# Six decay tiles spread by one-hot products into PSUM, products of zeros first, and a new order in the opening of an attention-then-FFN kernel

## The chip, the cores and the metric

One NeuronCore of a Trainium2 chip runs the whole program. The metric is device microseconds of one execution: the median of three runs before is 554.11 us (554.05 to 554.75). TensorE (PE) multiplies into PSUM, VectorE (DVE) and ScalarE (ACT) read and write SBUF and PSUM, GpSimd (POOL) works in SBUF, and SyncE (SP) issues nearly all transfers (DMAs), in the order of its queue.

## The reference

Three stages follow one another on 4 batches of 768 tokens:

1. A scan attention with 8 heads, 32 channels a head and a state of 16. With the decay `a` clipped to 1e-6..1, within a chunk `y[i] = sum over j<=i of (C_i . B_j) * prod(a[j+1..i]) * x_j`, plus `C_i . state` decayed to i; the state at the end of a chunk is the decayed old state plus the decayed sum of `B_j x_j`.
2. A first FFN on 256 channels: `h = max(x@w1, x@w2, x@w3)` (768 wide), then `h @ w_out`.
3. A second FFN: `(sigmoid(x@w_gate) * (x@w_val)) @ w_out` (1536 wide), output in float32.

All inputs are float32 or, for the weights, float64; the weights arrive as pairs of 32-bit words and are turned on the chip into a high and a low part of reduced float32.

## The kernel before, in words

The attention runs in 64 steps. A step `k` is one chunk `c = k // 8` of 96 tokens and one group `g = k % 8` of four (batch, head) units. `attention(k)` (L321) does for its step: on ACT a masked copy of C (L327, only in the first 16 steps), four float32 products `s` on PE (L332; from step 16 on bf16 products, L335), then on POOL and DVE the multiplication of `s` and of `bx` with the decay into `mt` (L340, L347), then four products `y` on PE (L356), each 32 columns of the array wide. After every fourth step ACT and DVE write `xt_hi` and `xt_lo` (L366, L368) and DVE transposes the new state into `xs` of the next chunk (L372). The first 12 steps (`START`) form the opening: only when `xt` of step 11 is written can the first FFN begin, on 512 tokens at a time.

The decay of two steps is one tile `dec{n}` (n = k // 2) of 8 units by 97 values, the same on all 128 partitions. `load_decay` (L267) transfers it from DRAM with a broadcast over the partitions, for n = 0 and 1 straight from the input, from n = 2 on from `ad`, a DRAM copy that `clip_all` (L256) has clipped and stored. Then `decay(n)` (L283) makes it into products of decays by two scans on DVE (L291), which multiply along each row and add the pattern `delta`, a constant of zeros and ones in PSUM (a copy of `delta_s` in SBUF). Four tiles exist at a time (`DECS`), so the transfer of tile n waits in SP's queue until the steps of tile n - 4 are done.

The weights of the first FFN come in twelve pieces (a00 to a51) of two 256 KB transfers. `BEHIND` says how many pieces are put in SP's queue behind the transfer of which decay tile. Each piece is decoded (L155 on) by three ACT instructions (L165, L170, L174), one on DVE (`t_a`, L178), two on POOL (L183, L213) and one more on ACT (L211).

The order on each engine is made by a planner that places instructions by its own estimate of when they are ready and by their order in the program; `tc.issue_after(i)` sets an instruction behind another on the same engine. `Pipe.tick` moves every open step and every open decode one stage on. In the first FFN a pass over 512 tokens has six blocks m (a piece pair each) of 18 products `u` and 6 products `o` (L406 to L408), 144 products of 512 columns in all; the steps 12 to 23 of the attention are spread over the first pass. In them the products `y` of four steps are issued together after the fourth (L353).

## Time and profile before

| | before |
|---|---|
| median of 3 runs | 554.11 us |
| time of the profiled execution | 554.77 us |
| its span, first to last instruction | 553.0 us |
| outside the span | 1.77 us |
| PE busy | 535.5 us (97%) |
| DVE, ACT, POOL busy | 384.0, 322.2, 128.2 us |
| moved by DMA | 50.5 MB |

All stretches named below are in microseconds from the start of the span. "Busy" is the time that instructions of an engine cover; the ends of PE's products are modelled, so its pace is best read from the distance between starts. PEclk is the granted TensorE clock as a share of 2.4 GHz; where the profile has no record of it, as in the first 43 us, the column shows 1.00. "PEld" is the loading of weights into PE's array, which overlaps the products. "x8" is the number of instructions that a row has merged.

### The profile page before, as it was taken

To read this page: it belongs to the slowest core of one execution; us is meant where nothing else is said; L and a number is where in the kernel's file an instruction comes from. 1 tells how busy PE (TensorE), PEld (TensorE's weight loads), DVE (VectorE), ACT (ScalarE), POOL (GpSimd) and SP (SyncE) were. 2 spreads that over 40 slices of the span, in tenths; PEclk is the share of its full clock that TensorE was granted. 3 is DMA by queue.
4 is the path that set the end of the run, shared out by engine and by line. 5 is a ranking of instruction groups with operands and counts; after the bars stand their busy time and mean duration, and the time that the engine had idled before them with its cause. 6 is when DMAs were issued, how large, how long until landed. Compare 5 with 4: busy or idle time off the path is not lost.

```text
span 553.0 us, 7923 instructions
## 1 busy us (share of the span) xinstructions
PE 535.5 (97%) x2885; PEld 429.3 (78%) x2885; DVE 384.0 (69%) x648; ACT 322.2 (58%) x571; POOL 128.2 (23%) x161
## 2 busy tenths in 40 slices
PE   5998999999999999999999999999999999999997
PEld 5777667777677778888888878877888878888885
DVE  4988985676776834799988896586455567554554
ACT  5667745334335223687798886675555565555563
POOL 3568996555555430000000000000000000000000
PEclk9999899999999999999999999999999999999999
DMA  7999985894985118013220000001000002000002
GB/s 234 344 268 241 298 200 87 187 180 142 192 197 125 31 59 321 1 38 118 76 75 0 1 1 2 0 19 58 1 0 2 0 1 77 0 1 0 1 0 76
DMA packets 32150, 50.51 MB, mean 91 GB/s; under 512 B 3184, under 2 KB 18160, under 8 KB 32112
## 3 DMA queue, kind: packets, MB, share of 16 engines
q1 hardware_dynamic: 31824, 49.63, 34.1%
q8 instruction: 22, 0.36, 0.3%
q10 hardware_dynamic: 288, 0.39, 0.2%
q14 instruction: 16, 0.13, 0.1%
HBM read 38.51 MB, written 3.25 MB: 76 GB/s over the span
## 4 chain that ended last, share of the span: by engine, by line
PE 83%; DMA 9%; DVE 4%; ACT 1%; issue 1%; SPq 0%; DVEq 0%; ACTq 0%
PE o L659 17%; PE ug L628 15%; PE uv L628 15%; PE u L406 9%; PE u L408 8%; PE u L407 8%; DMA raw_a<-in_w 6%; PE o L407 3%; PE o L406 3%; PE o L408 3%; DMA dec<-ad 2%; PE y L356 2%; PE s L335 1%; DVE dec L291 1%; DMA ad<-ac 1%
## 5 line engine op out<-in xcount | busy, mean ns | idle before, releaser
L659 PE MATMUL o<-hi,w_d 128*128 128x512 f32 x288 | 97.6, 390 | 0.0
L406 PE MATMUL u<-xt_hi,w_a 128*128 128x512 f32 x216 | 88.4, 409 | 3.7 <-DVE s L488 2.6
L628 PE MATMUL ug<-xt_hi,w_g 128*128 128x512 f32 x252 | 91.5, 392 | 0.1
L628 PE MATMUL uv<-xt_hi,w_v 128*128 128x512 f32 x252 | 90.3, 390 | 0.0
L407 PE MATMUL u<-xt_lo,w_a 128*128 128x512 f32 x216 | 85.8, 397 | 0.1
L408 PE MATMUL u<-xt_hi,w_a 128*128 128x512 f32 x216 | 85.5, 396 | 0.0
L659 PEld LDWEIGHTS o<-hi,w_d 128*128 128x128 f32 x288 | 54.0, 188 | 11.3 <-ACT hi L702 0.2
L703 DVE TENSOR_TENSOR lo<-y,hi 128x512 fp32r<-128x512 f32 x72 | 49.4, 688 | 16.8 <-ACT hi L702 15.9
L291 DVE TENSOR_TENSOR_SCAN dec<-dec,delta 128x388 f32<-128x388 f32 x64 | 57.8, 945 | 1.3 <-DMA dec<-ad 1.1
L477 ACT CAST hi<-s 128x512 fp32r<-128x512 f32 x36 | 22.3, 621 | 61.5 <-DVE s L488 60.9
L659 PE MATMUL o<-lo,w_d 128*128 128x512 f32 x144 | 56.4, 391 | 0.8 <-DVE lo L703 0.8
L628 PEld LDWEIGHTS ug<-xt_hi,w_g 128*128 128x128 f32 x252 | 47.3, 188 | 12.1 <-ACT ug L631 0.9
L628 PEld LDWEIGHTS uv<-xt_hi,w_v 128*128 128x128 f32 x252 | 47.3, 188 | 10.6 <-DVE y L699 0.8
L406 PEld LDWEIGHTS u<-xt_hi,w_a 128*128 128x128 f32 x216 | 41.2, 191 | 13.7 <-POOL mt L340 1.7
L628 PE MATMUL ug<-xt_lo,w_g 128*128 128x512 f32 x126 | 49.1, 390 | 0.0
L628 PE MATMUL uv<-xt_lo,w_v 128*128 128x512 f32 x126 | 49.0, 389 | 0.0
L408 PEld LDWEIGHTS u<-xt_hi,w_a 128*128 128x128 f32 x216 | 41.4, 192 | 9.1
L407 PEld LDWEIGHTS u<-xt_lo,w_a 128*128 128x128 f32 x216 | 41.3, 191 | 8.4 <-DVE xt_lo L368 0.6
L702 ACT CAST hi<-y 128x512 fp32r<-128x512 f32 x72 | 44.4, 620 | 5.8 <-DVE y L699 4.4
L699 DVE TENSOR_TENSOR y<-uv,y 128x512 f32<-128x512 f32 x36 | 24.8, 688 | 30.9 <-PE uv L628 30.7
L486 DVE TENSOR_TENSOR s<-u,s 128x512 f32<-128x512 f32 x36 | 24.8, 688 | 24.6 <-PE u L408 19.4
L636 DVE TENSOR_TENSOR y<-ug,y 128x512 f32<-128x512 f32 x36 | 24.8, 690 | 24.4 <-ACT y L633 17.4
(103 smaller groups left out, 956.9 us busy)
## 6 DMA issues: line engine op xcount, KB each, us to landing
dec<-ad SPq DMA_DIRECT2D x30, 388.0 KB, 5.8
raw_a<-in_w SPq DMA_DIRECT2D x18, 256.0 KB, 6.9
bi<-parts SPq DMA_DIRECT2D x36, 128.0 KB, 5.3
cs<-parts SPq DMA_DIRECT2D x36, 96.0 KB, 5.5
xs<-in_xh SPq DMA_DIRECT2D x6, 512.0 KB, 5.0
raw_g<-in_wg SPq DMA_DIRECT2D x6, 512.0 KB, 5.0
raw_v<-in_wv SPq DMA_DIRECT2D x6, 512.0 KB, 5.9
raw_d<-in_wo SPq DMA_DIRECT2D x6, 512.0 KB, 4.3
```

Source lines behind the costliest of these rows:

```text
L291: dve.tensor_tensor_scan(out=f, data0=f, data1=delta.rearrange("p u w -> p (u w)"), initial=0.0, op0=ALU.mult, op1=ALU.add)
L406: pe.matmul(ps, wlo, a_hi(k), start=k == 0, stop=False)
L407: pe.matmul(ps, whi, a_lo(k), start=False, stop=False)
L408: pe.matmul(ps, whi, a_hi(k), start=False, stop=k == kn - 1)
L477: act.copy(hl[0], s)
L486: dve.tensor_tensor(out=s, in0=banks[1], in1=s, op=ALU.max)
L628: turn[0] = pe.matmul(ps, w, x, start=new and e == 0, stop=e == 2, skip_group_check=not new)
L636: evict[1] = dve.tensor_tensor(out=self.t[k], in0=ps, in1=self.t[k], op=ALU.add)
L659: turn[0] = pe.matmul(acc2[t][d], w, x, start=n == 1 and e == 0, stop=n == M2 and e == 2)
L699: evict[1] = dve.tensor_tensor(out=g, in0=v, in1=g, op=ALU.mult)
L702: act.copy(hl[0], g)
L703: dve.tensor_tensor(out=hl[1], in0=g, in1=hl[0].bitcast(F32), op=ALU.subtract)
```

## The change

The six first decay tiles are no longer transferred. The decay input is loaded once, 64 rows of 4 units by 97 values into `a4`, and clipped; the other 64 rows are set to zero. `spread(h)` multiplies `a4` on PE by a matrix that is a column of `delta_s` with a single 1 in row h, the same for all 128 outputs, so that all 128 partitions of a PSUM bank hold row h of `a4`, half a decay tile. Two banks (`o0`, `o1`) are used in turn; product h + 2 follows the scan of h. The scan then reads this bank and `delta_s` and writes the tile in SBUF. Twelve products of zeros stand first on PE; eight more are written into the program behind steps 9, 10 and 11 (3, 3 and 2).

In the order: no transfer of tiles 0 to 5; the store of `ad` after the first `x`; two weight pieces right after the first transfers, then two behind each of tiles 6 to 10; the second half of `x` of chunk 1 and the `bc` of chunk 2 behind piece a01; tiles 6 and 7 are scanned after step 11 and after the DVE instruction of piece a10; the state's transposes of step 7 come after `xt_lo` of step 11; the DVE instructions of pieces a00, a01 and a10 are set behind the multiplications of steps 6, 7 and 11, those of the later pieces behind `xt_lo` of step 11; and in steps 12 to 23 each step issues its own products `y` (`SHARED` in place of `START`).

```diff
+LATER = START // 2
+IDLE0 = 12
+IDLE = {9: 3, 10: 3, 11: 2}
+AFTER = {"a00": 6, "a01": 7, "a10": 11}
+SPREAD = 6
-BEHIND = {4: 1, 5: 1, 6: 2, 7: 2, 8: 2, 9: 1, 10: 1, 11: 1, 12: 1}
+BEHIND = {6: 2, 7: 2, 8: 2, 9: 2, 10: 2}
...
-        with behind(1):
-            dve.scalar_tensor_tensor(out=t, in0=f1, scalar=3, in1=sg, op0=ALU.logical_shift_left,
-                                     op1=ALU.bitwise_or)
+        with behind(1) if second else tc.issue_after(mts[AFTER.get(name, -1)].ins):
+            mts[name] = dve.scalar_tensor_tensor(out=t, in0=f1, scalar=3, in1=sg,
+                                                 op0=ALU.logical_shift_left, op1=ALU.bitwise_or)
...
-        t = awk.tile([128, 2, LW], F32, tag="ac", bufs=1, name="ac")
+        t = a4[0:NC * NP * 2]
+        dve.memset(a4[NC * NP * 2:128], 0.0)
         sp.dma_start(out=t.rearrange("p u w -> p (u w)"),
-                     in_=ah.rearrange("r (s w) -> (r s) w", s=4))
+                     in_=ah.rearrange("r (s w) -> (r s) w", s=2))
...
+    def spread(h):
+
+        ps = pso.tile([128, TT], F32, tag=f"o{h % 2}", name=f"spread{h}")
+        pe.matmul(ps[:, 0:4 * LW], delta_s[:, 3, h + 1:h + 2].to_broadcast([128, 128]),
+                  a4.rearrange("p u w -> p (u w)"), start=True, stop=True)
+        spreads.append(ps)
+
+    def load_decay(n):
         t = awk.tile([128, PU, LW], F32, tag="dec", bufs=DECS, name=f"dec{n}")
-        i = sp.dma_start(out=t.rearrange("p u w -> p (u w)"), in_=src[n].partition_broadcast(128))
         dec[n] = t
+        if n < SPREAD:
+            return
+        i = sp.dma_start(out=t.rearrange("p u w -> p (u w)"), in_=ad[n].partition_broadcast(128))
...
-        if clip:
-            dve.tensor_scalar(out=t[:, :, 1:LW], in0=t[:, :, 1:LW], scalar1=1e-6, scalar2=1.0,
-                              op0=ALU.max, op1=ALU.min)
         for h in range(PU // 4):
             f = t[:, 4 * h:4 * h + 4].rearrange("p u w -> p (u w)")
-            dve.tensor_tensor_scan(out=f, data0=f, data1=delta.rearrange("p u w -> p (u w)"),
+            a, d = (spreads.pop(0)[:, 0:4 * LW], delta_s) if n < SPREAD else (f, delta)
+            dve.tensor_tensor_scan(out=f, data0=a, data1=d.rearrange("p u w -> p (u w)"),
                                    initial=0.0, op0=ALU.mult, op1=ALU.add)
+            if 2 * n + h + 2 < 2 * SPREAD:
+                spread(2 * n + h + 2)
...
-        sp.dma_start(out=r, in_=bch[:, c])
+        with tc.issue_after(mts["load a01"].ins):
+            sp.dma_start(out=r, in_=bch[:, c])
...
-        for i in [g] if k < START else (g, g - 3, g - 2, g - 1) if g % 4 == 3 else []:
+        for i in [g] if k < SHARED else (g, g - 3, g - 2, g - 1) if g % 4 == 3 else []:
...
-            dve.tensor_tensor(out=lo, in0=src, in1=hi.bitcast(F32), op=ALU.subtract)
-            if c + 1 < NC:
...
+            i = dve.tensor_tensor(out=lo, in0=src, in1=hi.bitcast(F32), op=ALU.subtract)
+            if k + 1 == START:
+                mts[-1] = i
+                with tc.issue_after(i.ins):
+                    turn(0, 1, ys[1])
+            if c + 1 < NC and k != 7:
+                turn(c, h, y)
...
-        elif k < 9:
-            decay(n + 1, n == 0)
-        else:
-            for i in ([n + 1] if k == 9 else []) + [n + 2]:
-                if i < NC * NP:
-                    with tc.issue_after(last[0].ins) if k > FIRST else ExitStack():
-                        decay(i)
+        elif k < START:
+            if n + 1 < LATER:
+                decay(n + 1)
+        elif n + 2 < NC * NP:
+            with tc.issue_after(last[0].ins):
+                decay(n + 2)
+
+    def idle_products(n, after=None):
+
+        ps = pso.tile([128, TT], F32, tag="o1", name=f"idle{after}")
+        z = sgs[1].rearrange("p b n -> p (b n)") if after is None else (
+            delta_s.rearrange("p u w -> p (u w)"))
+        z = z.bitcast(BF16)
+        for _ in range(n):
+            with tc.issue_after(mts[after].ins) if after is not None else ExitStack():
+                pe.matmul(ps, z[:, 0:128], z[:, 0:TT], start=True, stop=True)
...
+    idle_products(IDLE0)
     sp.dma_start(out=pk, in_=pick)
...
-    load_decay(0, ah)
+    for n in range(4):
+        load_decay(n)
     constants()
+    for h in range(2):
+        spread(h)
+    load_x(0, slice(0, 16))
     next(store_all, None)
-    load_x(0, slice(0, 16))
-    load_decay(1, ah)
-    load_decay(2, ad)
     load_x(0, slice(16, 32))
     sp.dma_start(out=bcf[1], in_=bch[:, 1])
-    load_decay(3, ad)
     load_x(1, slice(0, 16))
-    load_decay(4, ad)
-    decay(0, clip=True)
+    load_weights()
+    load_weights()
+    load_decay(4)
+    decay(0)
...
+        if k == 10:
+            weights_tick()
+            weights_tick()
+        if k - LEAD - 1 in IDLE:
+            idle_products(IDLE[k - LEAD - 1], k - LEAD - 1)
...
+    for n, name in enumerate((-1, "a10")):
+        with tc.issue_after(mts[name].ins):
+            decay(LATER + n)
```

## Rows read from the trace of the kernel before

**Rows 1.** Part 4 of the page: shares of the chain that ended last, by engine.

```profile
PE 83%; DMA 9%; DVE 4%; ACT 1%; issue 1%; SPq 0%; DVEq 0%; ACTq 0%
```

**Rows 2.** Windows: length, then busy us (count) by engine, PEclk, DMA share, GB/s.

```profile
14.00:36.00 22.00, 21.42 (x160) 17.01 (x154) 18.90 (x32) 14.32 (x26) 11.56 (x16) 1.00 1.06 309
36.00:56.00 20.00, 17.64 (x110) 14.06 (x110) 17.50 (x26) 14.42 (x25) 17.35 (x17) 1.00 1.01 257
56.00:82.00 26.00, 24.31 (x169) 17.96 (x170) 23.07 (x39) 16.12 (x27) 26.00 (x26) 0.93 0.94 247
```

**Rows 3.** Chain of waits in order of time, 0 to 60: start, length, what.

```profile
17.07 5.46 DMA dec<-ad
...
46.53 6.87 DMA raw_a<-in_w
```

**Rows 4.** Timeline of the weight loads, 14 to 17.3: start, length, instruction, [idle before].

```profile
14.34 1.78 PEld L332 LDWEIGHTS s<-y 128*128 128x128 f32 x8 [0.33 <-ACT y L327]
16.29 0.20 PEld L356 LDWEIGHTS y<-mt,xs 128*32 128x32 f32 x8 [0.17 <-POOL mt L340]
```

**Rows 5.** Timeline of PE, 39 to 45.

```profile
39.10 0.80 PE L407 MATMUL u<-xt_lo,w_a 128*128 128x512 f32 x1
...
42.68 0.57 PE L407 MATMUL u<-xt_lo,w_a 128*128 128x512 f32 x1
43.09 0.39 PE L408 MATMUL u<-xt_hi,w_a 128*128 128x512 f32 x1
43.32 1.03 PE L332 MATMUL s<-y 128*128 128x96 f32 x8
44.13 0.48 PE L406 MATMUL u<-xt_hi,w_a 128*128 128x512 f32 x1
```

**Rows 6.** Timeline of PE, 47 to 61.

```profile
49.03 1.13 PE L332 MATMUL s<-y 128*128 128x96 f32 x8 [0.98 <-DVE s L488]
...
53.34 0.97 PE L356 MATMUL y<-mt,xs 128*32 128x112 f32 x32
...
56.50 0.58 PE L406 MATMUL u<-xt_hi,w_a 128*128 128x512 f32 x1 [1.56 <-DVE s L488]
...
60.22 0.40 PE L408 MATMUL o<-hi,w_a 128*128 128x512 f32 x1
```

**Rows 7.** Timeline of PE, 149 to 151.

```profile
149.96 0.40 PE L356 MATMUL y<-mt,xs 128*32 128x112 f32 x8
150.29 0.73 PE L406 MATMUL o<-hi,w_a 128*128 128x512 f32 x2
```

**Rows 8.** Groups of DVE by line, 0 to 40: total us, mean ns, idle before.

```profile
L291 DVE TENSOR_TENSOR_SCAN dec<-dec,delta 128x388 f32<-128x388 f32 x16 | 14.5, 947 | 1.2 <-DMA dec<-ad 1.1
...
L372 DVE STREAM_TRANSPOSE xs<-y 32x128 f32<-32x128 f32 x8 | 2.5, 310 | 0.1
L368 DVE TENSOR_TENSOR xt_lo<-y,xt_hi 128x384 fp32r<-128x384 f32 x3 | 1.6, 541 | 0.0
```

**Rows 9.** Timeline: DVE at steps 11 and a10, POOL and PE near 80.

```profile
33.81 0.56 DVE L347 TENSOR_TENSOR mt<-s,dec 128x384 f32<-128x384 f32 x1 [1.90 <-PE s L332]
...
36.06 0.69 DVE L178 SCALAR_TENSOR_TENSOR t_a<-raw_a,sg 128x512 int32<-128x512 int32 x1
...
78.25 1.28 POOL L213 TENSOR_TENSOR w_a<-r_a,w_a 128x512 fp32r<-128x512 f32 x1
...
80.00 1.29 POOL L213 TENSOR_TENSOR w_a<-r_a,w_a 128x512 fp32r<-128x512 f32 x1
...
81.52 0.39 PE L406 MATMUL u<-xt_hi,w_a 128*128 128x512 f32 x1
```

**Rows 10.** Timeline, the first 10 us.

```profile
0.74 0.99 POOL L142 MEMSET sg<- 128x512 int32 x2 [0.29 <-POOLq L767]
...
6.65 7.22 PE L332 MATMUL s<-y 128*128 128x96 f32 x32 [6.65 <-DMA y<-in_bch]
```

**Rows 11.** DMA issues of 0 to 62: count, KB each, median us to landing.

```profile
dec<-ad SPq DMA_DIRECT2D x11, 388.0 KB, 6.4
```

More of the change, by code (lines that the diff above doesn't have):

```diff
@@ L134, in piece1 @@
         return wp1, wt1.setdefault(m, []), loads, f"a{m}{part}"
+    mts = {}
     todo = [(piece1, m, part) for m in range(M1) for part in range(2)]
@@ L149, in load_weights @@
         for k, s in enumerate(loads):
-            sp.dma_start(out=raw[:, 2 * k:2 * k + 2].rearrange("p b n t -> p b (n t)"), in_=s)
+            mts["load " + name] = sp.dma_start(
+                out=raw[:, 2 * k:2 * k + 2].rearrange("p b n t -> p b (n t)"), in_=s)
         loaded.append((raw, wpool, blocks, name))
@@ L254, in scan_attention_then_ffn @@
     pk = acon.tile([128, NG], F32, name="pk")
+    a4 = acon.tile([128, 4, LW], F32, name="a4")
     def clip_all():
-        t = awk.tile([128, 2, LW], F32, tag="ac", bufs=1, name="ac")
+        t = a4[0:NC * NP * 2]
+        dve.memset(a4[NC * NP * 2:128], 0.0)
         sp.dma_start(out=t.rearrange("p u w -> p (u w)"),
-                     in_=ah.rearrange("r (s w) -> (r s) w", s=4))
+                     in_=ah.rearrange("r (s w) -> (r s) w", s=2))
         dve.tensor_scalar(out=t[:, :, 1:LW], in0=t[:, :, 1:LW], scalar1=1e-6, scalar2=1.0,
@@ L263, in clip_all @@
         yield
-        sp.dma_start(out=ad.rearrange("r (s w) -> (r s) w", s=4),
+        sp.dma_start(out=ad.rearrange("r (s w) -> (r s) w", s=2),
                      in_=t.rearrange("p u w -> p (u w)"))
-    def load_decay(n, src):
+    spreads = []
+    def spread(h):
[4 more added lines that the diff above has]
+    def load_decay(n):
         t = awk.tile([128, PU, LW], F32, tag="dec", bufs=DECS, name=f"dec{n}")
-        i = sp.dma_start(out=t.rearrange("p u w -> p (u w)"), in_=src[n].partition_broadcast(128))
         dec[n] = t
+        if n < SPREAD:
+            return
+        i = sp.dma_start(out=t.rearrange("p u w -> p (u w)"), in_=ad[n].partition_broadcast(128))
         for _ in range(BEHIND.get(n, 0)):
@@ L346, in attention @@
         else:
-            last[0] = dve.tensor_tensor(out=m[:, :, 0:CH], in0=ps[:, :, 0:CH], in1=dc[:, :, 1:LW],
+            last[0] = mts[k] = dve.tensor_tensor(out=m[:, :, 0:CH], in0=ps[:, :, 0:CH], in1=dc[:, :, 1:LW],
                                         op=ALU.mult)
@@ L367, in attention, with turn @@
             yield
-            dve.tensor_tensor(out=lo, in0=src, in1=hi.bitcast(F32), op=ALU.subtract)
-            if c + 1 < NC:
-                for q in range(4):
-                    rows = slice(32 * q, 32 * q + 32)
-                    dve.transpose(
-                        out=xs[c + 1][rows, 16 * h:16 * h + 16, :].rearrange(
-                            "p (g q) d -> p g q d", q=4)[:, :, q, :],
-                        in_=y[rows, :, CH:128])
+            i = dve.tensor_tensor(out=lo, in0=src, in1=hi.bitcast(F32), op=ALU.subtract)
[5 more added lines that the diff above has]
+                turn(c, h, y)
+    def turn(c, h, y):
+        for q in range(4):
+            rows = slice(32 * q, 32 * q + 32)
+            dve.transpose(
+                out=xs[c + 1][rows, 16 * h:16 * h + 16, :].rearrange(
+                    "p (g q) d -> p g q d", q=4)[:, :, q, :],
+                in_=y[rows, :, CH:128])
     def prepare(k):
@@ L387, in prepare @@
             if 5 <= n + 4 < NC * NP:
-                load_decay(n + 4, ad)
-        elif k < 9:
-            decay(n + 1, n == 0)
-        else:
-            for i in ([n + 1] if k == 9 else []) + [n + 2]:
-                if i < NC * NP:
-                    with tc.issue_after(last[0].ins) if k > FIRST else ExitStack():
-                        decay(i)
+                load_decay(n + 4)
+        elif k < START:
[12 more added lines that the diff above has]
+                pe.matmul(ps, z[:, 0:128], z[:, 0:TT], start=True, stop=True)
     def att_step(ahead=0):
@@ L532, in scan_attention_then_ffn @@
             att_step(LEAD)
-        if k == 4:
-            load_x(1, slice(16, 32))
+        if k == 6:
+            with tc.issue_after(mts["load a01"].ins):
+                load_x(1, slice(16, 32))
         pipe.tick()
+        if k == 10:
[3 more added lines that the diff above has]
+            idle_products(IDLE[k - LEAD - 1], k - LEAD - 1)
     for _ in range(9):
```

2 lines of the change are left out of this document (1 added, 1 removed).

## The prediction

> **What bounds the kernel now.** I read the chain of waits first, since PE is busy 97% of the span and a busy share alone does not say what a stretch is waiting for. The chain is 83% PE and 9% DMA [rows 1], so the transfers end something, but only in one place: read in order of time, the chain is almost all transfers from 17.07, a decay tile, to 53.40, a weight transfer that starts at 46.53 and takes 6.87 us [rows 3]. From there on it is products. The opening is therefore the only part where anything but PE's own work is to be gained, and I cut it by windows [rows 2]. From 14 to 36 PE is busy 21.4 of 22 us and DMA is full (1.06). From 36 to 56, in the first FFN pass, PE loses 2.4 us, POOL is busy 17.35 of 20, and DMA is still full. From 56 to 82 POOL is busy all 26.00 us with decoding.
>
> PE's level in the opening is read from distances. Two products of 512 columns at 42.68 and earlier start 0.43 us apart (from 39.10 to 43.09 there are nine steps, 3.99 us), then 0.23 [rows 5]: 512 columns in 0.43 us is the 1.2 GHz level, in 0.23 us the 2.4 GHz level. So PE ran at half through the whole attention opening and rose only after some 4 us of such products; PEclk shows 1.00 there because the profile holds no record yet. At half, a step costs 1.78 + 0.17 + 0.20 + 0.33 = 2.48 us [rows 4], and nine such steps make up the stretch from 14 to 36. So three limits lie close together: PE at half in the opening, full DMA until 53.4, POOL's decoding until 81.3.
>
> **The change part by part.** All sums are against the profiled execution, 553.0 us of span and 554.77 us of time; the median is 0.66 us below that, and I take the gain off the median.
>
> *Zeros first.* The memset of the zeros ends at 1.73 [rows 10]. Twelve products of 512 columns at 0.43 us end at 6.8, and the first real product started at 6.65 [rows 10], so they cost about 0.2 us. They are as dense as the products after which the level rose at 43.1 and 60.2 [rows 5, 6], so I expect 2.4 GHz from about 6.
>
> *Spreads.* Twelve float32 products of 388 columns. No row has one. Nearest: four float32 products of 96 columns take 0.81 us at full level (43.32 to 44.13) [rows 5], 0.20 each, and by columns 388/96 x 0.20 = 0.82; the lower bound is the reduced float32 kind, 0.23 x 388/512 x 2 instructions = 0.34. I take 0.75, nearer the same type. At half level it would be 4.04 x 1.78/4 = 1.8 at most.
> The Trainium skill, "FP8 and Floating Point Precision", section "TensorE Precision Notes", says that true FP32 makes four passes through the array. That would be 4 x 388 / 2.4 = 0.65 us (an estimate from that page), 1.2 us less over twelve; the sum would come out near 547. The four short products of the row are a little slower than that rule, and the sum goes by the row.
>
> *The opening on PE, at full level.* 14 groups `s` (two run ahead) x 0.81 = 11.3; 12 groups `y` x 0.42 (0.33 from its start to the next product, and 0.09 more than the usual step before it) [rows 7] = 5.0; 12 spreads 9.0; six of the eight later zeros 1.4. From 6.8 that is 33.5 for the last `y`. Then `xt_hi` and `xt_lo` at about 0.54 each [rows 8]: first full products at 34.6 in place of 39.10 [rows 5]. **4.5 us.**
> DVE has less: 12 scans x 0.95, 12 multiplications x 0.55, two `xt_lo`, four transposes x 0.31, two decode instructions x 0.7 to 1.1 [rows 8, 9] = 22 us, from about 7.7, when the first spread is there, to 30. It hides under PE. The clips of tiles 0 and 1 go at no gain for the same reason. That the scan now takes its first operand from PSUM and its second from SBUF I cost at nothing: it already read one from each. Bounds: 0.55, the multiplication of the same size that reads PSUM and SBUF, to 1.1 per scan; DVE would then need 18 to 24 us, still under PE's 27. A spread waits for the scan of its bank; behind it on PE stand the `s` and `y` of the same step. With two banks that is 0; one bank late by a scan each time would be 10 x 0.95 = 9.5 us (a rival below).
>
> *Products at half level in the first pass.* Nine steps from 39.10 to 43.09 and nine from 56.50 to 60.22 [rows 5, 6] take 3.99 and 3.72 us in place of 2.04: **3.6 us** if PE stays at full level.
>
> *Transfers.* Six tiles of 388 KB [rows 11] leave a queue that is full, and the two first weight pieces stand before them all. The last transfers of pieces wait for tile 10, thus for step 13 at about 40, where now a weight on the chain lands as late as 53.40 [rows 3]. The late weights cost PE its waits for DVE's `s` at 49.03 and 56.50, 1.0 + 1.6 [rows 6]: DVE stood at a decode instruction whose piece had not landed. **2.6 us.** Store of `ad`, second half of `x`, `bc` and tiles 6 to 10 come later in SP's queue, behind 1 MB of weights; they are needed after step 11, with over 10 us to go, so 0.
>
> *Single groups y in steps 12 to 23.* 12 x 0.42 in place of 3 groups of 32 at about 1.0 (0.97 long) [rows 6, 7]: **-2.0 us.**
>
> *DVE at the start of the pass.* Tiles 6 and 7 (four scans, 3.8 us) and four transposes (1.2 us) now stand behind `xt_lo` of step 11 [rows 8], together with all decoding from a11 on, before the `s` that free PE's banks. DVE is busy 17.5 of 20 us there now [rows 2]. Bounds 0 and 5.0; I take **-1.5.**
>
> PE's side: 4.5 + 3.6 + 2.6 - 2.0 - 1.5 = 7.2 us.
>
> *POOL's side.* The second pair of pieces starts when the DVE instruction of a10 is done, behind step 11's multiplication: 33.81 + 0.56, then 36.06 [rows 9]. In the changed kernel that multiplication ends just before the last `y`, about 32.8: a shift of 3.2. Half of POOL's 2.65 idle us between 36 and 56 [rows 2] is filled as the pieces no longer come late: 1.3. The first piece of the last block is done at 78.25 + 1.28 = 79.53 and PE uses it from 81.52 [rows 9]: 2.0 of slack. 3.2 + 1.3 + 2.0 = 6.5 us is the most that POOL lets through.
>
> Two limits of 7.2 and 6.5 take turns at being late; I take off 0.5: a gain of 6.0. After the first pass the work is the same, and the start of the second pass carries to the end. **554.1 - 6.0 = 548.1 us.**
>
> **The rivals.**
> *A, the level falls back.* After the zeros PE works in pieces: a spread, a group of narrow products, a wait for the scan of a bank. For it: from 14 to 36 PE was busy all the time by the windows and never rose [rows 2]; and products of 512 columns at 56.50 run at half again after a stretch of `y`, small `s` and a wait of 1.56 us [rows 6]. Against it: spreads are wide, 0.75 of each 2 us, and zeros follow where the spreads end. Price: a step at half costs 0.97 more for `s`, 0.28 for `y`, 0.85 for its spread, 2.1 us in all. The gain of 6 is used up at three steps by PE's side alone, at the fifth if the earlier weights take every later wait away. Six steps: about 556. All twelve: first products at 60, and 42 us of pass (144 x 0.23, 5 of `s`, 5 of `y`) end at 102 in place of 88: about 568.
> The Trainium skill, "TensorE: Matmul & The Clock Gate", section "A second HAM failure mode: psum-queue depth-cycling", tells of just this: a kernel that cycles through PSUM banks idles briefly between groups, and its clock swings between the two levels. The fall at 56.5 agrees in kind; no row here has a spread.
> *B, DVE becomes the bound of the pass.* The 5 us of scans and transposes behind `xt_lo`, and decoding beside a busy POOL, hold back the `s` that PE waits for. For: DVE's 17.5 of 20 [rows 2]. Against: steps 12 and 13 need only tile 6. Price: another 4 us: gain 2, about 552.
> *C, the planner's order undoes it*, a bank waiting for its scan each time: 9.5 us more in the opening against the 6: within a few tenths of now, or slower by up to 3.
> *D, more.* Spreads near 0.5, no loss at DVE: opening 3 us shorter: 544.
>
> **How the numbers follow.** The forecast has 0.58 with its own range 545 to 551; B 0.15 (551 to 553.5); D 0.07 (below 545); A 0.14 (slower, 555 to 568); C 0.06, half no change, half slower. A change of 0.2%, 1.1 us, is about what a measurement of this kernel can tell. Faster: 0.58 + 0.15 + 0.07 = 0.80. Same: 0.03 of C and 0.01 of A's edge, 0.04. Slower 0.16. The range leaves out the worse part of A (0.10) and the better part of D (0.04): 543.5 to 556.5.
>
> **What would show it.** Right: products of 512 columns 0.23 us apart from the first FFN product on; `s` groups of eight 0.8 us long from about 7 on; spreads of 0.6 to 0.8 us; the first `xt_lo`-fed product near 34.6; last weight transfer issued near 40; POOL's last L213 near 76; second pass from about 82. Wrong if `s` groups in the opening take 1.8 us (A), if PE waits over 3 us in all for `s` between 35 and 60 (B), or if PE waits before spreads (C).

## The result: slower by 0.6%, where 1.1% faster was forecast

The changed kernel takes 558.83 us (median of 16 runs) against 554.88 us for the kernel before on the same chip (16 runs): a ratio of 1.0059, 95% interval 1.0039 to 1.0079. One of the 16 executions of the changed kernel took 3025.64 us and is left out of the ratio. The prediction of 548.1 is missed by 10.7 us, and the time lies above the forecast range of 543.5 to 556.5. One profiled execution of the changed kernel (span 556.8, time 558.86) is read here; single executions lie up to some 3 us from their median, so verdicts go by the medians, and profiles show only where a wait is.

**The loss is there when the second FFN pass begins.** The 145th product `u` (or `o`) of 512 columns is the first of the second pass. The timeline of PE puts it at 88.04 before:

```profile
88.04 0.48 PE L406 MATMUL u<-xt_hi,w_a 128*128 128x512 f32 x1
```

and at 92.01 in the changed kernel:

```profile
92.01 0.48 PE L444 MATMUL u<-xt_hi,w_a 128*128 128x512 f32 x1
```

From there to the end of the span it is 465.0 and 464.8 us. So all of it, 4.0 us in these two profiles, arises before 92 us.

**The opening.** The same windows as [rows 2], and two more (length, busy us and count of PE, PEld, DVE, ACT, POOL, then PEclk, DMA share, GB/s), in the changed kernel:

```profile
14.00:36.00 22.00, 18.66 (x153) 11.33 (x152) 15.04 (x25) 15.63 (x26) 11.01 (x14) 1.00 0.86 218
36.00:56.00 20.00, 14.54 (x85) 9.54 (x80) 15.88 (x28) 10.94 (x19) 13.61 (x16) 0.74 1.03 239
56.00:82.00 26.00, 26.00 (x193) 17.82 (x192) 21.87 (x38) 17.69 (x31) 26.00 (x25) 1.00 0.93 233
36.60:40.00 3.40, 3.18 (x14) 1.32 (x15) 2.01 (x5) 1.45 (x3) 1.50 (x2) 0.50 1.05 266
...
46.80:53.60 6.80, 3.51 (x15) 2.15 (x15) 5.38 (x11) 3.26 (x6) 4.33 (x6) 0.50 0.95 228
```

The transfers did make room: DMA's share falls from 1.06 to 0.86 between 14 and 36, and POOL is busy 13.61 us in place of 17.35 between 36 and 56. But PE lost 5.5 us in the second window in place of 2.4, and the last two rows show the level at half twice. How the opening's 22 us are spent stands in the timeline of PE (start, length, instruction; a float32 product is two instructions, so `x2` is one spread, `s` x8 and `y` x8 are groups of four):

```profile
16.56 0.39 PE L377 MATMUL y<-mt,xs 128*32 128x112 f32 x4
16.87 0.92 PE L281 MATMUL spread<-a,delta_s 128*128 128x388 f32 x2
17.72 0.39 PE L377 MATMUL y<-mt,xs 128*32 128x112 f32 x4
18.04 1.13 PE L353 MATMUL s<-y 128*128 128x96 f32 x8
19.10 0.38 PE L377 MATMUL y<-mt,xs 128*32 128x112 f32 x2
19.41 0.92 PE L281 MATMUL spread<-a,delta_s 128*128 128x388 f32 x2
...
27.21 0.40 PE L377 MATMUL y<-mt,xs 128*32 128x112 f32 x8
27.57 0.92 PE L281 MATMUL spread<-a,delta_s 128*128 128x388 f32 x2
28.32 1.03 PE L353 MATMUL s<-y 128*128 128x96 f32 x8
29.28 0.40 PE L377 MATMUL y<-mt,xs 128*32 128x112 f32 x8
...
31.34 0.84 PE L281 MATMUL spread<-a,delta_s 128*128 128x388 f32 x2
32.95 0.66 PE L377 MATMUL y<-mt,xs 128*32 128x112 f32 x16 [0.76 <-POOL mt L361]
35.74 0.40 PE L377 MATMUL y<-mt,xs 128*32 128x112 f32 x8 [2.13 <-DVE mt L368]
...
41.43 0.58 PE L445 MATMUL u<-xt_lo,w_a 128*128 128x512 f32 x1
```

A step is 2.54 us (16.87 to 19.41), no shorter than the 2.48 us of the kernel before, although that one ran at half level [rows 4] and this one at full. Where `y` is not split around a spread it is 2.07 (27.21 to 29.28). The first product fed by `xt_lo` starts at 41.43, 2.3 us later than before and 6.8 later than forecast.

**The start of the pass.** The chain on the page of the profile, against [rows 1]:

```profile
PE 86%; DMA 5%; DVE 4%; ACT 3%; issue 1%; SPq 1%; DVEq 0%; ACTq 0%
```

Two weight transfers of 5.4 and 5.6 us lie early in it, but its longest transfer, in order of time (start, length, what), is no longer a weight [rows 3] but the `x` of chunk 2:

```profile
37.87 10.26 DMA xs<-in_xh
```

DVE's timeline shows what stands behind it, and PE's that it waits 4.83 us for the last of DVE's rows:

```profile
48.15 1.29 DVE L401 STREAM_TRANSPOSE xs<-y 32x128 f32<-32x128 f32 x4 [2.51 <-DMA xs<-in_xh]
49.47 0.56 DVE L368 TENSOR_TENSOR mt<-s,dec 128x384 f32<-128x384 f32 x1
```

```profile
50.09 0.79 PE L444 MATMUL u<-xt_hi,w_a 128*128 128x512 f32 x1 [4.83 <-DVE mt L368]
```

DVE's rows stand in the order of its queue: transposes for chunk 2 wait for that chunk's buffer to be loaded, and the `mt` of step 12, for which chunk 2 is of no use yet, waits behind them.

### The profile page after: what moved, and what is told of

It reads as the page before. It is cut to its first block, busy times and chain, and to the rows that moved or that the text cites. A ratio compares the mean times of both kernels' runs of the same rounds, so it can differ in the third digit from the quotient of the medians.

```text
span 556.8 us, 7972 instructions
## 1 busy us (share of the span) xinstructions
PE 540.1 (97%) x2928; PEld 422.8 (76%) x2929; DVE 380.7 (68%) x647; ACT 322.3 (58%) x571; POOL 126.7 (23%) x161
## 4 chain that ended last, share of the span: by engine, by line
PE 86%; DMA 5%; DVE 4%; ACT 3%; issue 1%; SPq 1%; DVEq 0%; ACTq 0%
PE o L709 17%; PE ug L678 15%; PE uv L678 15%; PE u L444 9%; PE u L446 8%; PE u L445 8%; PE o L444 3%; PE o L445 3%; PE o L446 3%; PE y L377 2%; DMA raw_a<-in_w 2%; DMA xs<-in_xh 2%; PE s L356 2%; DVE dec L309 1%; DMA a<-in_ah 1%
## 5 line engine op out<-in xcount | busy, mean ns | idle before, releaser
L444 PE MATMUL u<-xt_hi,w_a 128*128 128x512 f32 x216 | 88.3, 409 | 5.2 <-DVE mt L368 4.8
L309 DVE TENSOR_TENSOR_SCAN dec<-dec,delta 128x388 f32<-128x388 f32 x52 | 46.8, 943 | 0.0
L683 ACT COPY sv<-uv 128x512 f32<-128x512 f32 x36 | 21.1, 587 | 33.4 <-PE uv L678 33.3
```

Of the source, the lines that this page charges most:

```text
L309: dve.tensor_tensor_scan(out=f, data0=a, data1=d.rearrange("p u w -> p (u w)"), initial=0.0, op0=ALU.mult, op1=ALU.add)
L444: pe.matmul(ps, wlo, a_hi(k), start=k == 0, stop=False)
L683: evict[0] = act.copy(self.temp(1 if i == 6 else 2), ps)
```

## Experiments

Each row of the table is a median against the kernel before on the same chip in the same rounds; the last columns are read from one profile each: the first product fed by `xt_lo`, and the 145th product. A difference of a few microseconds between two such profiles is not yet one between two kernels: the openings of before_single and before_lo_dve have the same instructions in the same order on PE, DVE, ACT and POOL as that of the kernel before, and end 2.1 and 1.7 us earlier in their profiles.

| run | median | ratio [95%] | xt_lo | 145th |
|---|---|---|---|---|
| kernel before | 554.88 | 1 | 39.1 | 88.0 |
| changed kernel | 558.83 | 1.0059 [1.0039, 1.0079] | 41.4 | 92.0 |
| spread_twice | 569.46 | 1.0254 [1.0215, 1.0292] | 48.7 | 103.4 |
| spread_r2 | 557.91 | 1.0050 [1.0027, 1.0073] | 37.6 | 89.7 |
| before_zeros | 559.00 | 1.0071 [1.0047, 1.0096] | 41.6 | 92.5 |
| x2_first | 561.78 | 1.0115 [1.0083, 1.0147] | 41.6 | 95.3 |
| decode_late | 564.79 | 1.0173 [1.0143, 1.0202] | 41.4 | 97.8 |
| turn_late | 559.70 | 1.0096 [1.0079, 1.0113] | 42.1 | 93.4 |
| turn_late7 | 559.82 | 1.0091 [1.0066, 1.0116] | 41.5 | 95.3 |
| turn_spread4 | 559.09 | 1.0086 [1.0067, 1.0105] | 42.1 | 91.9 |
| group_y | 561.49 | 1.0129 [1.0105, 1.0152] | 41.6 | 94.7 |
| before_single | 554.44 | 1.0010 [0.9985, 1.0034] | 37.0 | 85.3 |
| lo_dve | 562.26 | 1.0126 [1.0092, 1.0161] | 42.2 | 93.4 |
| before_lo_dve | 555.39 | 0.9996 [0.9978, 1.0015] | 37.4 | 85.9 |
| r2_turn_lo | 560.57 | 1.0090 [1.0065, 1.0115] | 39.2 | 95.3 |
| r2_turn | 554.48 | 1.0002 [0.9983, 1.0021] | 36.1 | 84.7 |
| r2_turn7 | 554.94 | 0.9999 [0.9983, 1.0015] | 37.2 | 86.9 |
| r2_turn_zeros | 556.61 | 1.0029 [1.0014, 1.0044] | 37.9 | 87.9 |
| r2_turn_nozeros | 555.73 | 1.0019 [0.9996, 1.0043] | 37.6 | 88.3 |
| r2_turn_spread5 | 556.65 | 1.0027 [1.0007, 1.0046] | 38.8 | 89.3 |

### Is it PE's work that sets the opening?

**spread_twice**, every spread computed twice:

```diff
-        pe.matmul(ps[:, 0:4 * LW], delta_s[...], a4..., start=True, stop=True)
+        for _ in range(2):
+            pe.matmul(ps[:, 0:4 * LW], delta_s[...], a4..., start=True, stop=True)
```

> The changed kernel with each of the twelve spreads issued twice into the same bank (double work, same result). Theory (PE's own work, spread 0.85 of 2.54 us per step, sets the opening): each extra product of 388 columns adds 0.65 us or more to a step, ten to twelve of them 6.5 to 8 us to the opening's end, 48 to 49 for the first xt_lo-fed product. Rival (VectorE or the round trip through the bank sets the opening, PE has slack in each step): under 3 us. The whole time rises by up to the same, less where decoding is late anyway.

The opening ends 7.3 us later than in the changed kernel. Its PE timeline gives the price of a spread too, two of them from 16.59 to 18.10, 0.75 us each:

```profile
16.59 1.57 PE L282 MATMUL spread<-a,delta_s 128*128 128x388 f32 x4
18.10 0.39 PE L378 MATMUL y<-mt,xs 128*32 128x112 f32 x6
```

So what a spread costs on PE is not hidden: the opening is bound by PE, as predicted, at a larger price a step.

**spread_r2**, each spread as two reduced-float32 products of a high and a low part, with a one-hot column of the same kind:

```diff
+    dve.tensor_copy(a4h, a4)
+    dve.tensor_tensor(out=a4l, in0=a4, in1=a4h.bitcast(F32), op=ALU.subtract)
...
+        for e, part in enumerate((a4l, a4h)):
+            pe.matmul(ps[:, 0:4 * LW], hot[:, h:h + 1].to_broadcast([128, 128]),
+                      part..., start=e == 0, stop=e == 1)
```

> The changed kernel with each spread made of two products of reduced float32 (high and low part of the decays, split on VectorE, added in PSUM) in place of one of full float32. Theory (PE's own work sets the opening at 2.54 us a step, 0.85 of it a spread): a spread takes 0.35 to 0.5 us, a step about 2.15, the first xt_lo-fed product comes 3 to 4.5 us before 41.43. The whole time falls by less, 1 to 3 us, as POOL's decoding bounds what follows; it begins earlier only by what the multiplication of step 11 gains. Rival (VectorE or POOL's multiplications bound the steps): the opening ends less than 1.5 us earlier.

PE's timeline: a spread is now 0.46 us (20.41 to 20.87; 0.52 ahead of a `y`), and two steps from `s` to `s` take 3.52 (18.64 to 22.16), 1.76 each:

```profile
18.64 1.13 PE L356 MATMUL s<-y 128*128 128x96 f32 x8
...
20.41 0.44 PE L284 MATMUL spread<-a4l,hot 128*128 128x388 f32 x1
20.69 0.34 PE L284 MATMUL spread<-a4h,hot 128*128 128x388 f32 x1
20.87 1.03 PE L356 MATMUL s<-y 128*128 128x96 f32 x8
21.83 0.40 PE L380 MATMUL y<-mt,xs 128*32 128x112 f32 x8
22.16 1.13 PE L356 MATMUL s<-y 128*128 128x96 f32 x8
```

The opening is 3.9 us shorter, but the ratio is only 0.0009 better, inside both intervals. The opening was one limit; "Both limits at once" below looks for the other.

### Does the level hold, and because of what?

**before_zeros**, the kernel before with the twelve first products of zeros alone:

```diff
+    z = sgs[1].rearrange("p b n -> p (b n)").bitcast(BF16)
...
+    for _ in range(12):
+        pe.matmul(ps, z[:, 0:128], z[:, 0:TT], start=True, stop=True)
     sp.dma_start(out=pk, in_=pick)
```

> The kernel before with twelve products of zeros first and nothing else. Theory (the level of the clock is what the zeros buy, spreads and order aside): TensorE runs at 2.4 GHz from about 6 us on, a step of the opening falls from 2.48 to about 1.5 us of PE and VectorE with 1.5 us a step becomes its bound; the opening ends 3 to 5 us earlier, but the weights still land as before (chain of transfers until 53.4), so the time falls by 0 to 4 us. Rival (without wide products the level falls back within the opening): s groups of eight take 1.8 us again after some steps, time within 1 us of the kernel before.

It is 0.7% slower than the kernel before. Windows (columns as above) and two rows of its timeline of PE: the level rises, PE waits 3.35 us for the `mt` of the first tile, and the level is at half until 35.9:

```profile
5.20:12.00 6.80, 3.90 (x29) 3.04 (x27) 2.57 (x4) 3.05 (x7) 0.60 (x2) 1.00 0.88 308
12.00:35.90 23.90, 22.92 (x160) 18.77 (x164) 17.69 (x31) 10.74 (x18) 8.03 (x13) 0.50 0.96 321
```

```profile
12.98 1.99 PE L332 MATMUL s<-y 128*128 128x96 f32 x8 [3.35 <-DVE mt L347]
...
41.00 0.80 PE L406 MATMUL u<-xt_hi,w_a 128*128 128x512 f32 x1 [4.72 <-POOL w_a L213]
```

In this window PE is busy 96% of the time with products of 96 and 112 columns, and the level does not come back. With spreads between them, as in the changed kernel, it stays at full from 5.9 to 36.6. So early zeros alone bring nothing here. But the loss is not the level's alone: the last `y` of the opening ends only 0.9 us later than before (36.3 for 35.4), and then PE waits 4.72 us for the first weight, which POOL decodes 8 us later than before (L183 at 34.76 for 26.53), in another order of the planner's.

Nor is it shown that wide products are needed to hold the level. The profile of before_single (below) has the kernel before's opening, and in it the level is at full from 12.1 to 29.2 with products of 96 and 112 columns alone; in that of before_lo_dve from 10.5 to 27.6. The window of before_single, and the starts of two groups `s` on PE that are eight steps apart:

```profile
12.10:29.20 17.10, 11.96 (x134) 9.48 (x133) 16.74 (x26) 11.29 (x19) 8.28 (x13) 1.00 1.02 330
```

```profile
12.70 1.10 PE L332 MATMUL s<-y 128*128 128x96 f32 x8 [0.42 <-DVE mt L347]
...
28.75 1.62 PE L332 MATMUL s<-y 128*128 128x96 f32 x8 [2.36 <-ACT w_a L211]
```

So the same opening ran at half throughout in one profile and at full for 17 us in two others. At full a step takes 2.0 us (16.05 for eight), DVE is busy 98% of the time, and PE, busy 70%, mostly waits for it. The changed kernel's step at full, 2.54 or 2.07, is no shorter than this either.

### Which wait holds the pass?

**x2_first**, the `x` of chunk 2 put ahead of tile 8 and its weights in SP's queue:

```diff
+            if n == D:
+                mts[f"x{c}"] = i
...
+                with tc.issue_after(mts["x2"].ins) if n + 4 == 8 else ExitStack():
+                    load_decay(n + 4)
```

> The changed kernel with one difference: in SyncE's queue the transfer of tile 8 and the two weight pieces behind it stand after the x of chunk 2, not before it. Theory (x of chunk 2, issued at 37.87 behind three weight transfers and landed at 48.13, holds VectorE's transposes 2.51 us, and by them the multiplication that PE waits 4.83 us for): x lands near 42, the transposes no longer wait, PE's longest wait falls from 4.83 to at most 2.5 us, TensorE keeps 2.4 GHz or loses it for less time, and the time falls by 3 to 6 us against the changed kernel, to 553 to 556. Rival 1 (the 3.5 us of scans of tiles 6 and 7 ahead of that multiplication is what holds it, the transfer is incidental): under 1.5 us of gain. Rival 2 (the loss lies in the opening, which ends 2.3 us later than before; what follows is hidden by POOL's decoding): no change within 0.5 us.

This missed. `x` is issued only 0.3 us earlier (37.56), and the planner put the transposes ahead of the scans of tiles 6 and 7, so that DVE's timeline has a longer wait with more behind it; PE waits 5.48 us at 49.73:

```profile
45.86 1.29 DVE L403 STREAM_TRANSPOSE xs<-y 32x128 f32<-32x128 f32 x4 [4.79 <-DMA xs<-in_xh]
...
47.91 3.52 DVE L311 TENSOR_TENSOR_SCAN dec<-dec,delta 128x388 f32<-128x388 f32 x4
```

**decode_late**, no early decoding of a00 and a01 between the steps:

```diff
-AFTER = {"a00": 6, "a01": 7, "a10": 11}
+AFTER = {"a00": 11, "a01": 11, "a10": 11}
...
-        if k == 10:
-            weights_tick()
-            weights_tick()
```

> The changed kernel without the early decode: pieces a00 and a01 go into the decode with the others, their VectorE instructions behind the multiplication of step 11. Theory (POOL's decode of a00 from 31.35 stands ahead of its multiplication for step 7, this of y, of xt_hi, and of the scans that VectorE has behind xt_lo): the opening ends 2 to 3 us earlier, first xt_lo-fed product near 38.5 in place of 41.43; the decode itself is then some 5 us later, so the time stays within 2 us. Rival (PE alone sets the opening at 2.54 us per step and POOL is incidental): the opening's end moves by under 0.7 us and the kernel gets slower by 2 to 4 us as the decode comes later.

The `xt_lo` of step 11 came 2.7 us earlier (36.3 for 39.0), which shows that the early decoding delays the opening's end. The expectation names POOL; in the changed kernel ACT has its part too. Its `xt_hi` of step 7 stands behind six decoding instructions from 29.28 on, and DVE waits for it (timelines of ACT and DVE):

```profile
33.07 0.47 ACT L387 CAST xt_hi<-y 128x384 fp32r<-128x384 f32 x1
```

```profile
33.57 0.56 DVE L389 TENSOR_TENSOR xt_lo<-y,xt_hi 128x384 fp32r<-128x384 f32 x1 [1.85 <-ACT xt_hi L387]
```

In decode_late ACT writes this `xt_hi` at 31.37, 1.7 us earlier, and DVE does not wait for it. Then PE waited 3.72 us at 40.85 for the weight itself (`w_a`, POOL L220) and 7.11 later. Slower by 1.7%: the early decoding is worth more than it costs.

**turn_late**, **turn_late7** and **turn_spread4**: the transposes of steps 8 to 11 behind the `mt` of step 13; then tile 7's scans there too; or, with the transposes, four tiles by spreads in place of six:

```diff
-            if c + 1 < NC and k != 7:
+            if c + 1 < NC and k not in (7, 11):
                 turn(c, h, y)
...
+        if k == 13:
+            with tc.issue_after(last[0].ins):
+                turn(1, 0, ys[0])
...
-SPREAD = 6
+SPREAD = 4      # turn_spread4
```

(The edit for tile 7 is shown with r2_turn7 below.)

> The changed kernel with four VectorE transposes moved: the state of steps 8 to 11 is transposed into the x of chunk 2 after the multiplication of step 13, not before that of step 12. Theory (VectorE, an in-order queue, stands 2.51 us at these transposes for an x that lands at 48.13, PE waits 4.83 us behind it, POOL's decoding behind it is idle for 6.4 of 20 us between 36 and 56): PE's longest wait in the first pass falls to under 2 us, POOL's last decode ends near 80 in place of 83.6, the first pass ends 3 to 4.5 us earlier (87.5 to 89 in place of 92.0) and the time is that of the kernel before within 1.5 us. Rival (the first pass ends where it does since the opening ends 2.3 us late and POOL is saturated after it): under 1.5 us of gain against the changed kernel.

> As turn_late, and the two scans of tile 7 behind the multiplication of step 13 too, where it was ahead of that of step 12. Theory (what stands ahead of the multiplication of step 12 on VectorE is paid by PE one for one): 1.8 us less ahead of it, another 1 to 2 us off the first pass. Rival (POOL's decoding bounds the pass once the transposes are away): within 0.7 us of turn_late.

> As turn_late, with four tiles by products in place of six; tiles 4 and 5 are transferred from the clipped copy. Theory (PE's own work sets the opening at 2.54 us a step, 0.85 of it a spread): four spreads less, the opening ends 2.5 to 3.4 us earlier (first xt_lo-fed product near 38.5 in place of 41.4) unless a tile lands late; two transfers of 388 KB more put the weights some 2.5 us back. Time 1 to 3 us under turn_late. Rival (without the wide products the level falls back to 1.2 GHz before the opening ends, as it did at 12.0 in the kernel with zeros alone): the opening ends later, time 2 us or more over turn_late.

In turn_late the wait of 4.83 us is gone, and the ratio is none the better. Its profile says why in part: other waits came (0.88, 1.63, 0.60 and 1.04), and from the first `xt_lo`-fed product to the 145th they add up to 4.5 us in place of 4.9; with tile 7 moved they are 7.5. With four spread tiles PE waits 2.5 us at 19.75 behind the scan of a transferred tile, and 4.16 at 39.95 for an `xt_hi` that ACT writes behind a decoding instruction whose weight had not landed. The wait that looked costliest was handed on, not taken away.

**lo_dve** and **before_lo_dve**: the low part of the hidden rows in the first pass computed by DVE, not POOL, in the changed kernel and in the one before:

```diff
-            chain.add(stages(s, banks, hl, dve if t > NTT - 3 else pool))
+            chain.add(stages(s, banks, hl, dve if t > NTT - 3 or t == 0 else pool))
```

> The changed kernel with one instruction per block of the first pass moved from POOL to VectorE: the subtraction that makes the low part of the hidden row (1.29 us on POOL, about 0.7 on VectorE). Theory (POOL's decoding bounds the first pass: whatever was done to waits of PE or VectorE, the pass ended 4.5 to 8.4 us after POOL's last weight): four of these stand before POOL's last decode, 5 us of POOL; its last decode ends 2 to 5 us earlier (79 to 81.5 in place of 83.6), the first pass ends 2 to 4.5 us earlier and the time is 554.5 to 557. Rival (VectorE, the in-order queue in which decode, scans and maxima stand, bounds the pass): no gain, or up to 3 us slower.

> The same move in the kernel before. Theory (there too POOL bounds the first pass: 43.9 us busy of 44.5 between the second pair of pieces and the last): its last decode ends 2 to 5 us before 81.3 and the time falls by 2 to 4.5 us, to 550 to 552.5. Rival (the chain of transfers until 53.4 sets that pass, POOL only follows): within 1 us.

POOL's last decode comes 3.4 us earlier (80.2 for 83.6), and the changed kernel is slower still; before, the same edit makes no difference. So POOL's last decode does not set the end of the changed kernel's pass. The rival said that more work on DVE would hurt; the time agrees, but no run separates that from the order which the planner then chose.

**group_y** and **before_single** turn the single groups `y` of steps 12 to 23 around, off in the changed kernel and on in the one before:

```diff
-        for i in [g] if k < SHARED else (g, g - 3, g - 2, g - 1) if g % 4 == 3 else []:
+        for i in [g] if k < START else (g, g - 3, g - 2, g - 1) if g % 4 == 3 else []:
```

> The changed kernel with the products y of steps 12 to 23 issued four steps together, as before the change. Theory (each switch between wide products and a group of narrow ones costs PE 0.3 to 0.4 us, and nine groups more are 2 us of PE's pass): first pass 1 to 2 us shorter if PE bounds it. Rival (POOL's decoding bounds the first pass, the switches lie in waits): within 0.7 us of the changed kernel.

> The kernel before, with the groups y of steps 12 to 23 issued one by one and not four by four: the term of -2.0 us alone. As predicted it costs PE 12 groups of 0.42 in place of 3 of about 1.0: 2 us slower, a ratio near 1.004. Rival (what group_y suggests: groups of 32 hold back the xt that the FFN waits for, so single groups win back what they cost): same or faster.

With PE's waits left out and the steps at half level counted as at full, the stretch from the first `xt_lo`-fed product to the 145th is some 44.0 us in the changed kernel and 42.3 in group_y, an estimate from the distances between starts: single groups add 1.7 us, near the 2.0 forecast. But taking them away makes the changed kernel slower, as PE's waits there grow from 4.9 to 8.4 us, and adding them to the kernel before costs nothing that can be measured. The work is real and hidden.

### Both limits at once

In spread_r2 PE waits 2.97 us at 45.02 for `mt` of step 12. DVE's timeline from `xt_lo` on shows why without a transfer: it is never idle. Transposes, decoding and four scans stand ahead of it:

```profile
36.08 0.56 DVE L392 TENSOR_TENSOR xt_lo<-y,xt_hi 128x384 fp32r<-128x384 f32 x1 [2.57 <-ACT xt_hi L390]
36.56 1.28 DVE L404 STREAM_TRANSPOSE xs<-y 32x128 f32<-32x128 f32 x4
37.87 1.17 DVE L185 SCALAR_TENSOR_TENSOR t_a<-raw_a,sg 128x512 int32<-128x512 int32 x1
39.08 1.81 DVE L312 TENSOR_TENSOR_SCAN dec<-dec,delta 128x388 f32<-128x388 f32 x2
40.81 0.67 DVE L185 SCALAR_TENSOR_TENSOR t_a<-raw_a,sg 128x512 int32<-128x512 int32 x1
41.39 1.81 DVE L312 TENSOR_TENSOR_SCAN dec<-dec,delta 128x388 f32<-128x388 f32 x2
43.11 1.26 DVE L404 STREAM_TRANSPOSE xs<-y 32x128 f32<-32x128 f32 x4
44.41 0.56 DVE L371 TENSOR_TENSOR mt<-s,dec 128x384 f32<-128x384 f32 x1
```

**r2_turn** is spread_r2 with turn_late's edit; **r2_turn7** has tile 7's scans moved as well; **r2_turn_lo** is r2_turn with lo_dve's edit:

```diff
 # r2_turn = spread_r2 and turn_late; r2_turn7 also:
-    for n, name in enumerate((-1, "a10")):
-        with tc.issue_after(mts[name].ins):
-            decay(LATER + n)
+    with tc.issue_after(mts[-1].ins):
+        decay(LATER)
...
+                if k == 13:
+                    decay(LATER + 1)
```

> Spreads as two reduced-float32 products, and the transposes of steps 8 to 11 moved behind the multiplication of step 13, so that they no longer stand in DVE's queue ahead of the multiplication that PE waited 2.97 us for at 45.02 of spread_r2. Theory (the queue of DVE in front of that multiplication is what takes the gain back: 7.8 us of transposes, scans and decoding from 36.56 to 44.41): 2.5 us less queue, the wait of 2.97 shrinks to about 0.5, the level does not fall at 45, the 145th product of the first FFN at 86 to 88 in place of 89.7, the median near 555. Rival (the wait is only handed on, to the next product that needs DVE): the 145th product still at 89 to 91 and the median 557 to 559.

> As r2_turn, and tile 7's two scans too behind the multiplication of step 13: the queue in front of step 12's multiplication is 4.3 us shorter than in spread_r2. Theory: no wait over 1 us between 38 and 46, the 145th product at 85 to 87, the median 553 to 554.5, not slower than the kernel before. Rival (the wait is handed on: tile 7 is wanted by step 14, the scans stand ahead of its multiplication then): 89 to 91 and 557 to 559.

> Three edits at once on the changed kernel: the spreads of two reduced products, the transposes of steps 8 to 11 behind the multiplication of step 13, and the low part of the hidden row on VectorE in the first pass. Theory (opening by PE, then POOL's decoding, then VectorE's wait, each of which comes to the front when the one before is taken away): the first pass ends at 84 to 87 in place of 92.0 and the time is 549 to 552, under the kernel before. Rival (a later limit, PE's switches between narrow and wide products, takes most of it): 553 to 556.

r2_turn takes back the whole loss: 1.0002 against 1.0050 of spread_r2, intervals apart. Its DVE reaches the `mt` at 41.66, and PE's wait is 1.66 us, not the 0.5 expected; the level still falls there, for 3.4 us (its timelines of DVE and PE, from an execution 2.2 us under its median):

```profile
41.66 0.53 DVE L371 TENSOR_TENSOR mt<-s,dec 128x384 f32<-128x384 f32 x1
```

```profile
42.25 0.75 PE L450 MATMUL u<-xt_hi,w_a 128*128 128x512 f32 x1 [1.66 <-DVE mt L371]
```

r2_turn7 takes away that wait as well, and its level is at full through the whole pass, but it gains nothing more. Its profile shows other waits in the pass, 5.1 us in all against 2.8 in r2_turn, the longest of them for DVE again:

```profile
49.84 0.50 PE L452 MATMUL u<-xt_hi,w_a 128*128 128x512 f32 x1 [1.47 <-DVE s L534]
```

r2_turn_lo missed its forecast by far and is 0.9% slower than before: its level is at half from 27.4 to 37.7 and from 44.5 to 54.7. The first of these stretches lies in the opening, on which lo_dve's edit has no direct part, so this run does not tell what more work on DVE costs.

**r2_turn_zeros**, **r2_turn_nozeros** and **r2_turn_spread5** looked for a version that beats the kernel before: seven late zeros more, none of the eight late ones, or five spread tiles.

```diff
-IDLE = {9: 3, 10: 3, 11: 2}
+IDLE = {8: 3, 9: 3, 10: 3, 11: 6}     # r2_turn_zeros
+IDLE = {}                             # r2_turn_nozeros
-SPREAD = 6
+SPREAD = 5                            # r2_turn_spread5
```

> As r2_turn, with seven more products of zeros (three behind step 8, three more behind step 11). If the time hangs on the level falling after PE's waits in 30 to 46: no row at half between 30 and 46, about 1 to 2 us less than r2_turn. If the extra products only fill PE's queue: the first product fed by xt_lo is up to 1.6 us later than in r2_turn, and the time the same or more.

> r2_turn without the eight products of zeros at the end of the opening (the twelve first ones stay). If these hold the level: the products of the first FFN start at 0.43 us steps, up to 4 us longer, median 556 to 557. If they only fill PE's queue, as the slower r2_turn_zeros suggests: the first product fed by xt_lo 0.5 to 1.5 us earlier, median 553 to 554, about 0.2% faster than the kernel before.

> r2_turn with five tiles by one-hot products in place of six: four spread products fewer, and one transfer of 388 KB more, ahead of the weights. By the working that PE bounds the opening: 4 x 0.3 = 1.2 us less on PE, the first product fed by xt_lo near 35, the median 553 to 554. Rival: the transferred tile or the later weights are late: a wait before the scan of tile 5, median 555 to 557.

More zeros only delay the pass, 0.3% slower than before. Without the late ones the first FFN products do start at half level: in PE's timeline 0.43 us apart from 37.64 until 40.62.

```profile
37.64 0.63 PE L451 MATMUL u<-xt_lo,w_a 128*128 128x512 f32 x1
38.06 0.63 PE L452 MATMUL u<-xt_hi,w_a 128*128 128x512 f32 x1
...
40.62 0.47 PE L450 MATMUL u<-xt_hi,w_a 128*128 128x512 f32 x1
```

With them, in r2_turn, they start 0.23 us apart. So the eight zeros do there what they are there for, as far as one profile of each shows, but the ratios, 1.0002 and 1.0019, have overlapping intervals. With five spread tiles PE waits 3.51 us at 22.76, in the opening, behind DVE's scan of a transferred tile that was late: the rival's price was larger than the spreads saved. None of 18 kernels beats the kernel before.

## Why the prediction was wrong, by its steps

**What bounds the kernel, and zeros first: right for the profile read.** The level rises before 6 us and the first real product starts at 6.38 (6.8 forecast). But the gain was counted against one execution whose opening stood at half. In before_single and before_lo_dve the same opening ran at full for 17 us and ended at 37.0 and 37.4, DVE being busy all but 0.4 us of that stretch in the first: against such executions even the forecast 34.6 would have brought 2.4 to 2.8 us, not 4.5. How many executions of the kernel before are of this kind no trace tells.

**"The opening on PE, at full level": the step that failed**, 2.3 us later in place of 4.5 earlier: 6.8 of the 10.0 us between the 82 forecast for the second pass and the 92.0 measured. Two parts:
- *Price of a step, 3.2 us.* The last spread ends at 32.1. By then there are 12 groups `s`, 8 groups `y` and 12 spreads, which at the forecast's prices is 9.7 + 3.4 + 9.0 = 22.1 us from 6.8, thus 28.9. The spread itself was priced right (0.75 taken; 0.75 two in a row, 0.85 ahead of a `y`). What was not: the planner puts it into the middle of a group `y`, and then it is 0.85, `s` is 1.06 (0.96 elsewhere in the opening, 0.81 forecast) and the two halves of `y` take 0.63 (0.42). The price of `s` came from a row in which one group stands among products of 512 columns [rows 5]; among `y` of another shape it was dearer; why, no run shows.
- *The end of the opening, 3.6 us.* From the last spread to the first `xt_lo`-fed product it is 9.3 us in place of 5.7. PE waits 3.5 us of it: for POOL's `mt` behind an early decode, then for scans that stand on DVE behind the `xt_lo` of step 7, which waits for ACT behind the same decode (decode_late takes 2.7 us out of this). The prediction had checked DVE's sum for the opening, not the order on DVE, POOL and ACT at its end.

The Trainium skill, "FP8 and Floating Point Precision", section "TensorE Precision Notes", says that true FP32 makes four passes, from which the prediction estimated 0.65 us. The 0.75 measured in a row lies above it, as [rows 5] did, and the measurement decides.

**Products at half level: about 2 of the 3.6 us.** Rival A was right in kind at another place: the level held through the spreads but fell behind the wait of 2.13 and in that of 4.83 us. The level is at half for 6.8 us of the pass, but PE waits through 3.3 of them (to 50.09); products at half take the other 3.5 us, in place of 7.7 before (3.99 + 3.72). The Trainium skill, "TensorE: Matmul & The Clock Gate", section "A second HAM failure mode: psum-queue depth-cycling", speaks of a clock that swings as PE idles briefly and often between groups while it cycles through banks. The changed kernel's trace does not show this: while its spreads cycled through two banks the level did not fall (1.00 from 5.9 to 36.6), and the two falls stand at single long waits.

**Transfers: the 2.6 us of waits for weights did go, others came.** The first pass has 4.9 us of PE's waits in place of 3.9. The prediction put the transfers that now come later at 0 and does not name the `x` of chunk 2; issued at 37.87 in place of 35.79, it held DVE for 2.51 us. The prediction looked for the next limit on POOL; the long wait was on DVE.

**DVE at the start of the pass: -1.5 taken, 5.0 the bound, and the bound was nearer.** The wait was 4.83 us, and spread_r2 and r2_turn show it as the second limit: shortening the opening alone moves the ratio by 0.0009, moving the transposes alone (turn_late) by nothing to the good, both together by 0.0057. This is rival B's mechanism, and the term was too small, but 4.83 us was not its worth either: it shows only when the opening is shortened as well.

**Single groups `y`: 1.7 us for 2.0, right as work, wrong as time**, as group_y and before_single show. **POOL's side**: its last decode, forecast near 76, came at 83.6, but it is not the limit of the changed kernel (lo_dve).

What stays open: what makes a group dearer beside a spread; why the waits that turn_late and r2_turn7 removed came back at other places, for DVE's `s` among others (the profiles show that they did, but no run took them away); and how much of each difference is the planner's new order and not the edit.

## What to carry to other kernels

Price an added product in the order in which the planner will issue it: between groups of another shape the groups around it cost more, and a spread that is cheap alone made a step at full level as long as the old one at half. When a stage is pulled forward, list the in-order queue of every engine at its end, instruction by instruction; sums of busy time did not show that a multiplication would stand behind transposes waiting for a transfer. Read the start from more than one execution: here a stretch that stood at half level in one profile ran at full in two others. If removing the most visible wait brings nothing, look for a second limit of the same length and remove both at once before calling either harmless.

## What the runs showed of the hardware that was not expected

- Products of 96 and 112 columns ran at either level: PE was 96% busy with them for 23.9 us at half (before_zeros, 12.0 to 35.9), and 70% busy for 17.1 us at full (before_single, 12.1 to 29.2). With float32 products of 388 columns between them the level was at full for some 30 us (changed kernel, 5.9 to 36.6).
- A 388-column one-hot product in float32 took 0.75 to 0.85 us, in reduced float32 two of them, high and low part, took 0.46 to 0.52 together (spread_r2): the split saves more than a third.
- The level fell in or right behind PE waits of 2.13 and 4.83 us (changed kernel), 3.35 us (before_zeros) and 2.36 us (before_single), and the products that followed ran at half, so that such a wait cost more than its length.
